# Attention and two MoE layers on one core: transposes of the layer norm's input and of w3 on fp32r-typed operands

## The chip, the cores and the metric

The kernel runs on one core of a Trainium2 chip. The metric is the device time of one execution in microseconds (us), as the median over runs. A measurement of this kernel can tell about 0.3% (some 3.8 us) from no change.

## The reference

All inputs and outputs are float32 (the MoE weights arrive as float64 and are rounded to float32 by the kernel).

```python
def _attn_ref(q, k, v):                      # q, k, v: (8, 8, 576, 64)
    k_p = k.reshape(B, H, Sp, 8, D).mean(axis=3); v_p = ...   # pooled by 8
    attn = softmax(scale * q @ k_p^T)
    return attn @ v_p

def _moe_ref(x, w_in, w_out, g_ln):          # x: (4608, 512), w_in: (512, 1024)
    h = x @ w_in
    solu = h * softmax(h)
    ln = (solu - mean) / sqrt(var + 1e-06) * g_ln
    return ln @ w_out

def _moe2_ref(x, w1, w2, w3, w_out):         # w3: (1024, 1024)
    return ((x @ w1) * (x @ w2) @ w3) @ w_out
```

## The kernel before, in words

Three stages follow each other. TensorE multiplies most matrices as fp32r (one pass) after each fp32 operand has been split into a high and a low fp32r part, three products each; a few products and all transposes run on plain fp32 operands.

**Stage one (to about 640 us)** runs attention, the first MoE layer and the conversion of weights together. Work goes by units of 256 tokens, 18 in all (`Unit`, lines 617 to 655), each of two `Rows` of 128 tokens (lines 567 to 605). A row's product with w_in fills the PSUM tile `h` (`chunk`, line 588: 24 matmuls of 512 columns in four chunks of six). `exp` (line 592) writes the tile `e` (128x1024 fp32), `solu` (line 600) turns `e` on VectorE (line 603) into the layer norm's input, and ScalarE squares it for the variance (line 605). `Unit.transpose(i, hf)` (line 622) transposes half `hf` of row `i`: four 128x128 TensorE transposes of `e` into the PSUM tile `lt` (line 631), a ScalarE copy to `lnh` (line 634) and, one slot later, a VectorE subtraction to `lnl` (line 635). `Unit.chunk` (line 637) multiplies `lnh` and `lnl` with the second weight (lines 645 to 647, 256 columns each) into `x`, which `store` (line 651) copies to `xo` and sends to DRAM. The first quarter of that product needs half 0 of both rows, the second quarter half 1.

The order of stage one on TensorE and on SP, which issues every DMA, is the program's order: a table `events` holds functions by slot, 16 slots to a unit (`put`, `after`, lines 129 to 134; the loop at line 784). A slot's events run first, then one chunk of heavy work: row 0's `h` in slots 0 to 3, `x` in 4 to 7, row 1's `h` in 8 to 11, `x` in 12 to 15. The four transposes of unit u stand in slots 0 to 3 of the next 16 (line 738). VectorE, ScalarE and GpSimd get their order from the scheduler of the framework, which sets it when the program is built. SP issues in order and stands at a DMA whose data or buffer isn't ready. In the same slots the kernel rounds float64 weights, 128x512 at a time (`Rounded`, line 151): a load into `f64` (three buffers, line 157), `cvm` and `cvb` steps on ScalarE (line 170) and VectorE (lines 173 to 182), a sum on GpSimd, a store to DRAM (line 255). Of the attention's own work this text names `q` loads and their transposes `pq`, scores `sc`, exponentials `ea`, the transposes `pt` and `px` of the probabilities, and the product `av`.

**Stage two (about 642 to 710 us)** folds w3 into w_out2: `w3_T(m)` (line 850) loads two 128x512 pieces of w3 into `stg`, transposes each by four TensorE transposes into `pw` (line 857) and splits it; `wf_rows` (line 861) multiplies, 24 matmuls of 512 columns per m. **Stage three** does the second MoE layer and isn't touched.

Of the kernel before, what the change touches and what calls it, by code (L numbers as in the profile page):

```python
# [8 lines left out]
F32 = mybir.dt.float32  # L9
F32R = mybir.dt.float32r  # L10
I32 = mybir.dt.int32
U32 = mybir.dt.uint32
AF = mybir.ActivationFunctionType
# [5 lines left out]
def attention_moe_kernel(  # L19
# [25 lines left out]
    nc = tc.nc  # L45

    B, H, S, D = q.shape
    P = 128
    C = H * D
    NP = H // 2  # L50
    F = w_in.shape[1]
# [15 lines left out]
    const = ctx.enter_context(tc.tile_pool(name="const", bufs=1))  # L67
# [5 lines left out]
    def bank(name):  # L73
        return PS.tile([P, 512], F32, tag="ba", name=name, bufs=3)

    def bankm(name):
        return PS.tile([P, 512], F32, tag="bm", name=name, bufs=3)
# [4 lines left out]
    ident = const.tile([P, P], F32, tag="ident", name="ident")  # L82
    make_identity(nc, ident)
    negid = const.tile([P, P], F32R, tag="negid", name="negid")
    nc.scalar.activation(negid, ident, AF.Copy, scale=-1.0)

    mask8 = const.tile([P, H], F32, tag="mask8", name="mask8")
    m16 = const.tile([P, 16], F32, tag="m16", name="m16")
# [10 lines left out]
    def split(hi, lo, src):  # L99
        nc.scalar.activation(hi, src, AF.Copy)  # L100
        nc.vector.tensor_tensor(lo, src, hi.bitcast(F32), ALU.subtract)
# [7 lines left out]
    def piece(w, i, width=512):  # L109

        n = w.shape[1] // width
        return w[(i // n) * P : (i // n) * P + P, (i % n) * width : (i % n) * width + width]
# [10 lines left out]
    SLOTS = 16  # L123
# [5 lines left out]
    def put(slot, fn, *args, first=5):  # L129
        assert now is None or slot > now  # L130
        events.setdefault(slot, []).append((first, len(events.get(slot, ())), fn, args))

    def after(d, fn, *args, first=3):
        put(now + d, fn, *args, first=first)
# [16 lines left out]
    class Rounded:  # L151
# [7 lines left out]
        def words(self):  # L159
            return A.tile([P, 512, 2], I32, tag="f64", name="f64", bufs=3)  # L160
# [88 lines left out]
    f32w = {}  # L249
# [317 lines left out]
    class Rows:  # L567
# [32 lines left out]
        def solu(self):  # L600

            st, e = self.s, self.e
            nc.vector.scalar_tensor_tensor(e, self.hv, -1.0 / F, e, ALU.mult, ALU.mult, accum_out=st[:, 2:3])
            sq = M2.tile([P, F], mybir.dt.bfloat16, tag="sq", name="sq" + self.nm, bufs=1)
            nc.scalar.activation(sq, e, AF.Square, bias=st[:, 2:3], scale=-1.0 * F, accum_out=st[:, 3:4])

    def out_scale():

        s, ss = ST[:, :, 1], ST[:, :, 3]
        nc.vector.tensor_scalar(kap, s, 1e-9, None, ALU.add)  # L610
        nc.vector.tensor_tensor(kap, kap, kap, ALU.mult)
        nc.vector.tensor_scalar(kap, kap, LNEPS * F, None, ALU.mult)
        nc.vector.tensor_tensor(kap, kap, ss, ALU.add)
        nc.vector.tensor_scalar(kap, kap, 1.0 / F, None, ALU.mult)
        nc.vector.reciprocal(kap, kap)

    class Unit:
# [4 lines left out]
        def transpose(self, i, hf):  # L622
            if (i, hf) == (0, 0):
                self.th, self.tl = [
                    M2.tile([P, FC, U], F32R, tag=t, name=f"{t}{self.u}", bufs=1) for t in ("lnh", "lnl")
                ]
            ln = self.rows[i].e
            pt = bankm(f"lt{self.u}_{i}_{hf}")
            for f in range(4):
                f0 = (4 * hf + f) * P  # L630
                nc.tensor.transpose(pt[:, f * P : f * P + P], ln[:, f0 : f0 + P], ident)  # L631
            fs, cs = slice(4 * hf, 4 * hf + 4), slice(i * P, i * P + P)
            hi, lo, src = self.th[:, fs, cs], self.tl[:, fs, cs], pt.rearrange("p (f n) -> p f n", f=4)
            nc.scalar.activation(hi, src, AF.Copy)  # L634
            after(1, lambda: nc.vector.tensor_tensor(lo, src, hi.bitcast(F32), ALU.subtract), first=0)  # L635
# [30 lines left out]
    T0 = (8, 13)  # L666
# [66 lines left out]
    for un in units:  # L733
        s_ = SLOTS * un.u
        if un.u >= 2 * B:
            put(s_ - 4, un.rows[0].split_x)
        for n in range(4):
            put(s_ + SLOTS + n if un.u else T0[n % 2] + n // 2, un.transpose, n % 2, n // 2, first=1)

    mid = ExitStack()  # L740
    M2 = R = o2 = first_raw = first_w3 = None
# [22 lines left out]
    def w3_pair(m):  # L764
        return [R.tile([P, FC, P], F32R, tag="w3" + t, name=f"w3{t}{m}", bufs=2) for t in "hl"]
# [18 lines left out]
    with tc.manual_schedule(engines={mybir.EngineType.PE, mybir.EngineType.SP}):  # L784
        for s_ in range(min(events), SLOTS * (NU + 1) + 2):
# [3 lines left out]
            u, c = s_ // SLOTS, s_ % SLOTS  # L789
            kind, n = HEAVY[c], c % 4  # L790
# [59 lines left out]
    def w3_T(m):  # L850
        th, tl = w3_pair(m) if m else first_w3
        for i in range(2):
            t = R.tile([P, 512], F32, tag="stg", name="stg", bufs=4)
            nc.sync.dma_start(t, piece(f32w["w3f"], 2 * m + i))
            pw = bank(f"pw{m}_{i}")
            for c in range(4):
                nc.tensor.transpose(pw[:, c * P : c * P + P], t[:, c * P : c * P + P], ident)
            split(th[:, 4 * i : 4 * i + 4], tl[:, 4 * i : 4 * i + 4], pw.rearrange("p (c n) -> p c n", c=4))
        return th, tl

# [9 lines left out]

    BLOCKS_AT = (0, 2, 4, 5)
    nxt = w3_T(0)
    for m in range(FC):
        cur = nxt
        if m + 1 < FC:
            nxt = w3_T(m + 1)
        ow = wf_rows(m, cur)
        if m < FC - 1:
            split(wf[0][:, m], wf[1][:, m], ow)
        if m in BLOCKS_AT:  # L880
            i = BLOCKS_AT.index(m)
            split_blocks(i // 2, i % 2, load_blocks(i // 2, i % 2) if i else first_raw)
# [3 lines left out]
    M2 = ctx.enter_context(tc.tile_pool(name="mlpb", bufs=2, reuse_waits="tile"))  # L886
# [201 lines left out]
```

## Time and profile before

| | before |
|---|---|
| median of 3 runs | 1275.96 us (1274.64 to 1278.98) |
| the profiled execution | 1277.2 us |
| its span | 1275.4 us |
| TensorE matmul busy | 1230.8 us, 97% of the span |
| VectorE, ScalarE, GpSimd busy | 63%, 41%, 32% |
| mean granted TensorE clock | 0.994 |
| DMA | 109.43 MB, q1 busy 29.6% of 16 engines |

The span is the time between the first and the last instruction of the profiled execution; 1.8 us lie around it. The profile has a list of groups of instructions by line, a timeline in order of time, a list of waits (which engine stood still, and what ended that), and the chain: the work that ended last, followed back from the last instruction through whatever released each step. In tile names buffer numbers are left out (`e`, `lt`, `f`). Matmuls are pipelined, so a matmul's own duration is longer than its distance to the next one's start; what a matmul costs in a stream is that distance.

### The profile page before, as it was taken

Reading aid. Unit: us, or ns where it says so; the run is one execution under the profiler, and the core shown is the slowest. Engines: PE = TensorE matmul, PEld = TensorE weight load, DVE = VectorE, ACT = ScalarE, POOL = GpSimd, SP = SyncE. Lnnn points to the kernel's source line nnn. Section 1 sums busy time; section 2 is a strip of 40 time slices with the busy share of each in tenths; the row PEclk is TensorE's granted clock in tenths of the full one; section 3 lists DMA queues with packets and bytes.
Section 4 is the critical chain, followed back from the end, with each engine's and each line's share of the span. In section 5 each row is a group of like instructions: output and inputs, shape, how many; then the busy total and the mean of one; then the engine's idle time right before and its main releaser. Section 6 shows DMA issues by size and latency. Waiting matters only on the chain.

```text
span 1275.4 us, 21828 instructions
## 1 busy us (share of the span) xinstructions
PE 1230.8 (97%) x8278; PEld 1124.8 (88%) x8278; DVE 807.3 (63%) x1595; ACT 525.1 (41%) x1480; POOL 406.6 (32%) x497
## 2 busy tenths in 40 slices
PE   7879999999999999999999999999999999999998
PEld 5669889988988898998988899999999999999997
DVE  6879778777878787755357555545454545454544
ACT  5554666666656666644354221212121212121211
POOL 3332534342525253210000141515152424242411
PEclk9999999999999999999999999999999999999999
DMA  9564546454546464214033102010101010101000
GB/s 236 121 135 115 156 111 164 117 158 133 166 132 167 116 167 116 87 42 140 35 128 111 33 1 67 1 67 1 67 1 67 2 67 1 67 1 66 13 22 34
DMA packets 85754, 109.43 MB, mean 86 GB/s; under 512 B 43664, under 2 KB 43664, under 8 KB 85648
## 3 DMA queue, kind: packets, MB, share of 16 engines
q1 hardware_dynamic: 85648, 108.03, 29.6%
q8 instruction: 65, 1.06, 0.4%
q14 instruction: 41, 0.34, 0.1%
HBM read 78.65 MB, written 29.36 MB: 85 GB/s over the span
## 4 chain that ended last, share of the span: by engine, by line
PE 77%; DVE 9%; DMA 5%; ACT 5%; issue 2%; SPq 1%; POOL 0%; DVEq 0%; ACTq 0%; POOLq 0%
PE h L588 11%; PE p L948 9%; PE p L950 9%; PE p L949 9%; PE acc L994 5%; PE acc L997 5%; PE acc L996 5%; PE x L646 3%; PE x L647 3%; PE x L645 3%; DMA f<-in_moe_w_dram 3%; PE av L557 2%; PE lt L631 2%; ACT ea L473 2%; PE sc L452 1%
## 5 line engine op out<-in xcount | busy, mean ns | idle before, releaser
L968 POOL TENSOR_TENSOR a<-a,b 128x256 f32<-128x256 f32 x72 | 52.9, 735 | 477.5 <-DVE b L967 477.5
L952 ACT ACTIVATE p<-p 128x256 f32<-128x256 f32 x72 | 27.9, 387 | 397.4 <-PE p L950 365.4
L645 PE MATMUL x<-lnh,gwh 128*128 128x256 f32 x576 | 166.4, 289 | 0.0
L646 PE MATMUL x<-lnl,gwh 128*128 128x256 f32 x576 | 163.0, 283 | 2.1 <-DVE lnl L635 2.1
L647 PE MATMUL x<-lnh,gwl 128*128 128x256 f32 x576 | 162.8, 283 | 0.0
L189 POOL TENSOR_TENSOR cvb<-cvb,cvm 128x512 f32<-128x512 f32 x46 | 60.9, 1325 | 186.3 <-DVE cvm L182 180.6
L473 ACT ACTIVATE ea<-sc,mx 128x72 f32<-128x72 f32 x320 | 98.6, 333 | 36.7 <-DVE mx L470 36.7
L997 PE MATMUL acc<-wfl,ph 128*128 128x512 f32 x288 | 113.0, 393 | 0.0
L646 PEld LDWEIGHTS x<-lnl,gwh 128*128 128x128 f32 x576 | 110.1, 191 | 3.3 <-DVE lnl L635 2.3
L996 PE MATMUL acc<-wfh,ph 128*128 128x512 f32 x288 | 112.9, 392 | 0.0
L645 PEld LDWEIGHTS x<-lnh,gwh 128*128 128x128 f32 x576 | 110.0, 191 | 1.0 <-DVE lnl L635 0.2
L647 PEld LDWEIGHTS x<-lnh,gwl 128*128 128x128 f32 x576 | 110.0, 191 | 0.0
L967 DVE TENSOR_TENSOR b<-b,p 128x256 f32<-128x256 f32 x72 | 30.2, 419 | 123.0 <-PE p L950 123.0
L588 PE MATMUL h<-winh,xh 128*128 128x512 f32 x288 | 99.0, 425 | 0.0
L588 PE MATMUL h<-winl,xh 128*128 128x512 f32 x288 | 89.9, 393 | 0.0
L588 PE MATMUL h<-winh,xl 128*128 128x512 f32 x288 | 89.6, 392 | 0.0
L948 PE MATMUL p<-th,w1h 128*128 128x256 f32 x288 | 81.6, 283 | 1.1 <-ACT p L952 1.1
L994 PE MATMUL acc<-wfh,pl 128*128 128x512 f32 x288 | 82.3, 392 | 0.0
L635 DVE TENSOR_TENSOR lnl<-lt,lnh 128x512 fp32r<-128x512 f32 x72 | 49.2, 686 | 51.3 <-ACT lnh L634 50.9
L949 PE MATMUL p<-th,w1h 128*128 128x256 f32 x288 | 81.5, 283 | 0.0
L950 PE MATMUL p<-th,w1l 128*128 128x256 f32 x288 | 81.5, 283 | 0.0
L956 DVE TENSOR_TENSOR u<-p,p 128x256 f32<-128x256 f32 x72 | 30.3, 421 | 77.3 <-PE p L950 76.2
(201 smaller groups left out, 3725.1 us busy)
## 6 DMA issues: line engine op xcount, KB each, us to landing
f<-in_moe_w_dram SPq DMA_DIRECT2D x32, 512.0 KB, 5.8
x2d<-xo SPq DMA_DIRECT2D x36, 256.0 KB, 2.0
xq<-x2d SPq DMA_DIRECT2D x36, 256.0 KB, 3.7
out_dram<-ot SPq DMA_DIRECT2D x36, 256.0 KB, 2.7
kv<-in_k_dram SPq DMA_DIRECT2D x32, 256.0 KB, 3.7
q<-in_q_dram SPq DMA_DIRECT2D x32, 256.0 KB, 7.5
kv<-in_v_dram SPq DMA_DIRECT2D x32, 256.0 KB, 3.6
f<-in_moe_w_out_dram SPq DMA_DIRECT2D x16, 512.0 KB, 6.0
```

The lines of the kernel that those rows point to most:

```text
L189: self.engine.tensor_tensor(self.f, self.f, self.m.bitcast(F32), ALU.add)
L473: nc.scalar.activation(e[0:n, x], half[a][:, h], AF.Exp, bias=mx[0:n, x : x + 1], scale=1.0, accum_out=sm[0:n, x : x + 1],)
L588: nc.tensor.matmul(self.ph[:, a], s_[:, c], w_[:, c, a * 512 : a * 512 + 512], start=first, stop=last)
L645: nc.tensor.matmul(o, gw[0][:, f, ws], self.th[:, f], start=(f == 0), stop=False)
L646: nc.tensor.matmul(o, gw[0][:, f, ws], self.tl[:, f], start=False, stop=False)
L647: nc.tensor.matmul(o, gw[1][:, f, ws], self.th[:, f], start=False, stop=(f == FC - 1))
L948: nc.tensor.matmul(o, wh[:, c, fsl], th[:, c], start=c == 0, stop=False)
L949: nc.tensor.matmul(o, wh[:, c, fsl], tl[:, c], start=False, stop=False)
L950: nc.tensor.matmul(o, wl[:, c, fsl], th[:, c], start=False, stop=c == 1)
L994: nc.tensor.matmul(accs[t], pl[:, ts], wh, start=False, stop=(fc == FC - 1))
L996: nc.tensor.matmul(accs[t], ph[:, ts], wh, start=(fc == 0), stop=False)
L997: nc.tensor.matmul(accs[t], ph[:, ts], wl, start=False, stop=False)
```

## The change

The transposes of the layer norm's input and of w3 take fp32r-typed operands: a second identity, `identr`, is typed fp32r, and the transposes' outputs are viewed as fp32r. An operand typed fp32r has to come from a tile of that type. For w3 the staging tile itself is now typed fp32r and the load writes it through an fp32 view. The layer norm's input is written by VectorE in fp32 and is read by ScalarE for the variance; so each row gets a tile `er` (128x1024 fp32r, two buffers), filled from `e` by two DMAs of 128x512 (256 KB each) through an fp32 view, issued by SP one slot after `solu`: 72 DMAs of 18.9 MB together. The four transposes of a unit are reordered: row 0's two halves, then row 1's two, where before half 0 of both rows came first. The numbers of the transposes, copies and subtractions stay.

```diff
--- before.py
+++ after.py
@@ -83,6 +83,8 @@
     make_identity(nc, ident)
     negid = const.tile([P, P], F32R, tag="negid", name="negid")
     nc.scalar.activation(negid, ident, AF.Copy, scale=-1.0)
+    identr = const.tile([P, P], F32R, tag="identr", name="identr")
+    nc.scalar.activation(identr, ident, AF.Copy)
 
     mask8 = const.tile([P, H], F32, tag="mask8", name="mask8")
     m16 = const.tile([P, 16], F32, tag="m16", name="m16")
@@ -603,6 +605,14 @@
             nc.vector.scalar_tensor_tensor(e, self.hv, -1.0 / F, e, ALU.mult, ALU.mult, accum_out=st[:, 2:3])
             sq = M2.tile([P, F], mybir.dt.bfloat16, tag="sq", name="sq" + self.nm, bufs=1)
             nc.scalar.activation(sq, e, AF.Square, bias=st[:, 2:3], scale=-1.0 * F, accum_out=st[:, 3:4])
+            after(1, self.words, first=2)
+
+        def words(self):
+
+            self.er = M2.tile([P, F], F32R, tag="er", name="er" + self.nm, bufs=2)
+            for i in range(2):
+                cs = slice(i * 512, i * 512 + 512)
+                nc.sync.dma_start(self.er[:, cs].bitcast(F32), self.e[:, cs])
 
     def out_scale():
 
@@ -624,11 +634,11 @@
                 self.th, self.tl = [
                     M2.tile([P, FC, U], F32R, tag=t, name=f"{t}{self.u}", bufs=1) for t in ("lnh", "lnl")
                 ]
-            ln = self.rows[i].e
+            ln = self.rows[i].er
             pt = bankm(f"lt{self.u}_{i}_{hf}")
             for f in range(4):
                 f0 = (4 * hf + f) * P
-                nc.tensor.transpose(pt[:, f * P : f * P + P], ln[:, f0 : f0 + P], ident)
+                nc.tensor.transpose(pt[:, f * P : f * P + P].bitcast(F32R), ln[:, f0 : f0 + P], identr)
             fs, cs = slice(4 * hf, 4 * hf + 4), slice(i * P, i * P + P)
             hi, lo, src = self.th[:, fs, cs], self.tl[:, fs, cs], pt.rearrange("p (f n) -> p f n", f=4)
             nc.scalar.activation(hi, src, AF.Copy)
@@ -735,7 +745,7 @@
         if un.u >= 2 * B:
             put(s_ - 4, un.rows[0].split_x)
         for n in range(4):
-            put(s_ + SLOTS + n if un.u else T0[n % 2] + n // 2, un.transpose, n % 2, n // 2, first=1)
+            put(s_ + SLOTS + n if un.u else T0[n // 2] + n % 2, un.transpose, n // 2, n % 2, first=1)
 
     mid = ExitStack()
     M2 = R = o2 = first_raw = first_w3 = None
@@ -850,11 +860,11 @@
     def w3_T(m):
         th, tl = w3_pair(m) if m else first_w3
         for i in range(2):
-            t = R.tile([P, 512], F32, tag="stg", name="stg", bufs=4)
-            nc.sync.dma_start(t, piece(f32w["w3f"], 2 * m + i))
+            t = R.tile([P, 512], F32R, tag="stg", name="stgr", bufs=4)
+            nc.sync.dma_start(t.bitcast(F32), piece(f32w["w3f"], 2 * m + i))
             pw = bank(f"pw{m}_{i}")
             for c in range(4):
-                nc.tensor.transpose(pw[:, c * P : c * P + P], t[:, c * P : c * P + P], ident)
+                nc.tensor.transpose(pw[:, c * P : c * P + P].bitcast(F32R), t[:, c * P : c * P + P], identr)
             split(th[:, 4 * i : 4 * i + 4], tl[:, 4 * i : 4 * i + 4], pw.rearrange("p (c n) -> p c n", c=4))
         return th, tl
```

TensorE at the end of unit 5 and the start of unit 6 (`lt6_i_hf` is unit 6, row i, half hf; `h7_0` is row 0 of unit 7), before:

```order
L647 MATMUL x2_5_1_3347<-lnh5_3019,gwl_104 128x256
L631 MATMUL lt6_0_0_3449<-ident_66,e6_0_3140 128x128 x4
L588 MATMUL h7_0_3463<-winh_101,xh7_3284 128x512 x2
...
L631 MATMUL lt6_1_0_3471<-ident_66,e6_1_3317 128x128 x4
...
L631 MATMUL lt6_0_1_3501<-ident_66,e6_0_3140 128x128 x4
...
L631 MATMUL lt6_1_1_3515<-ident_66,e6_1_3317 128x128 x4
L518 MATMUL pt8_1_3521<-ident_66,pr8_1_3479 128x128 x4
```

and now:

```order
L657 MATMUL x2_5_1_3388<-lnh5_3057,gwl_106 128x256
L641 MATMUL lt6_0_0_3493<-identr_73,er6_0_3220 128x128 x4
L590 MATMUL h7_0_3507<-winh_103,xh7_3325 128x512 x2
...
L641 MATMUL lt6_0_1_3515<-identr_73,er6_0_3220 128x128 x4
...
L641 MATMUL lt6_1_0_3545<-identr_73,er6_1_3425 128x128 x4
...
L641 MATMUL lt6_1_1_3559<-identr_73,er6_1_3425 128x128 x4
L520 MATMUL pt8_1_3565<-ident_66,pr8_1_3523 128x128 x4
```

Row 1's first transpose has moved from the second to the third place; nothing else moved on TensorE.

SP in unit 5 (`e5_0` is row 0 of unit 5; `f64` a weight piece, `kv4` keys of the batch after), before:

```order
L655 DMA x2d_100<-xo3_1_2638 128x512
L426 DMA q7_1_2666<-in_q_dram 128x8x64
L157 DMA f64_2668<-in_moe2_w3_dram 128x1024
L255 DMA w3f_119<-cvb_2642 128x512
L429 DMA QL_115<-in_q_dram 64x8x64
L157 DMA f64_2762<-in_moe2_w3_dram 128x1024
L300 DMA kv4_0_2796<-in_k_dram 64x2x512 x2
L308 DMA KL8_117<-in_k_dram 64x1x512
L655 DMA x2d_100<-xo4_0_2828 128x512
```

and now:

```order
L665 DMA x2d_102<-xo3_1_2670 128x512
L428 DMA q7_1_2698<-in_q_dram 128x8x64
L159 DMA f64_2700<-in_moe2_w3_dram 128x1024
L257 DMA w3f_121<-cvb_2674 128x512
L431 DMA QL_117<-in_q_dram 64x8x64
L615 DMA er5_0_2787<-e5_0_2755 128x512 x2
L159 DMA f64_2797<-in_moe2_w3_dram 128x1024
L302 DMA kv4_0_2831<-in_k_dram 64x2x512 x2
L310 DMA KL8_119<-in_k_dram 64x1x512
L665 DMA x2d_102<-xo4_0_2863 128x512
```

The copy of row 0 stands ahead of a weight load and the key loads, which now wait with it for `e5_0`.

ScalarE around row 1 of unit 5, before:

```order
L440 ACTIVATE qT7_1_2873<-pq7_1_2868 128x512
L170 ACTIVATE cvm_3045<-f64_2881 128x512
L597 ACTIVATE e5_1_2898,ST_77<-h5_1_2841,ST_77 128x1024
L473 ACTIVATE ea7_1_2944,sm7_1_2943<-sc7_1_0_2907,mx7_1_2942 128x72 x4
L473 ACTIVATE ea7_1_2944,sm7_1_2943<-sc7_1_1_2910,mx7_1_2942 128x72 x2
```

and now:

```order
L172 ACTIVATE cvm_2922<-f64_2797 128x512
L475 ACTIVATE ea7_0_2885,sm7_0_2884<-sc7_0_0_2866,mx7_0_2883 128x72 x4
L475 ACTIVATE ea7_0_2885,sm7_0_2884<-sc7_0_1_2869,mx7_0_2883 128x72 x4
L442 ACTIVATE qT7_1_2908<-pq7_1_2903 128x512
L599 ACTIVATE e5_1_2933,ST_79<-h5_1_2876,ST_79 128x1024
L475 ACTIVATE ea7_1_2979,sm7_1_2978<-sc7_1_0_2942,mx7_1_2977 128x72 x4
```

The scheduler has moved the weight step that stood ahead of `e5_1` elsewhere, and put the one on `f64_2797` ahead of the exponentials `ea7_0`.

## Rows read from the trace of the kernel before

**Rows 1.** The page: the span.
```profile
span 1275.4 us, 21828 instructions
```
**Rows 2.** Busy time by stretch: us, PE (x), PEld, DVE, ACT, POOL, PEclk, DMA share, GB/s.
```profile
250.00:350.00 100.00, 97.77 (x680) 89.62 (x679) 79.71 (x149) 64.86 (x221) 46.20 (x61) 1.00 0.53 148
```
**Rows 3.** The chain that ended last, shares of the span by line.
```profile
PE h L588 11%; PE p L948 9%; PE p L950 9%; PE p L949 9%; PE acc L994 5%; PE acc L997 5%; PE acc L996 5%; PE x L646 3%; PE x L647 3%; PE x L645 3%; DMA f<-in_moe_w_dram 3%; PE av L557 2%; PE lt L631 2%; ACT ea L473 2%; PE sc L452 1%
```
**Rows 4.** Timeline of PE in unit 6: start us, us, engine, line, operation, count.
```profile
304.96 0.29 PE L647 MATMUL x<-lnh,gwl 128*128 128x256 f32 x1
305.09 0.60 PE L631 MATMUL lt<-ident,e 128*128 128x128 f32 x4
305.44 0.71 PE L588 MATMUL h<-winh,xh 128*128 128x512 f32 x2
305.99 0.63 PE L588 MATMUL h<-winl,xh 128*128 128x512 f32 x2
...
306.92 0.60 PE L631 MATMUL lt<-ident,e 128*128 128x128 f32 x4
...
308.74 0.60 PE L631 MATMUL lt<-ident,e 128*128 128x128 f32 x4
```
**Rows 5.** Groups of PE by line and shape: count, busy us, mean ns, idle before.
```profile
L452 PE MATMUL sc<-bdt,qT 128*128 128x144 f32 x320 | 48.1, 293 | 3.0 <-ACT qT L440 3.0
L631 PE MATMUL lt<-ident,e 128*128 128x128 f32 x288 | 43.8, 276 | 6.2 <-ACT qT L440 5.7 <-DVE lnl L635 0.6
```
**Rows 6.** Timeline of PE early in stage one.
```profile
15.31 0.33 PE L374 MATMUL pkl<-ident,KL 128*128 128x128 f32 x1
...
17.86 1.14 PE L452 MATMUL sc<-bdt,qT 128*128 128x144 f32 x8
```
**Rows 7.** Timeline of PEld, the loading of stationary operands, there.
```profile
15.31 0.14 PEld L374 LDWEIGHTS pkl<-ident,KL 128*128 128x128 f32 x1 [0.17 <-issue]
15.37 0.47 PEld L437 LDWEIGHTS pq<-ident,q 128*128 128x128 f32 x4
```
**Rows 8.** Timeline of PE: fp32r products of 320 columns.
```profile
295.09 0.31 PE L557 MATMUL av<-ptl,VBDh 128*128 128x320 f32 x1
295.24 0.31 PE L557 MATMUL av<-pth,VBDl 128*128 128x320 f32 x1
```
**Rows 9.** Timeline of PE at the start of stage two.
```profile
653.71 1.91 PE L857 MATMUL pw<-ident,stg 128*128 128x128 f32 x16
```
**Rows 10.** Timeline of DVE: the layer norm's input, rows 5_0, 6_1 and 17_1.
```profile
248.71 1.22 DVE L603 SCALAR_TENSOR_TENSOR e<-h,e 128x1024 f32<-128x1024 f32 x1
...
299.79 1.22 DVE L603 SCALAR_TENSOR_TENSOR e<-h,e 128x1024 f32<-128x1024 f32 x1
...
636.83 1.22 DVE L603 SCALAR_TENSOR_TENSOR e<-h,e 128x1024 f32<-128x1024 f32 x1
```
**Rows 11.** DMA issues: count, KB each, median us from issue to landing.
```profile
f<-in_moe_w_dram SPq DMA_DIRECT2D x32, 512.0 KB, 5.8
x2d<-xo SPq DMA_DIRECT2D x36, 256.0 KB, 2.0
```
**Rows 12.** Timeline of PE at the end of stage one, unit 17.
```profile
639.43 1.51 PE L631 MATMUL lt<-ident,e 128*128 128x128 f32 x12
...
642.09 0.39 PE L645 MATMUL x<-lnh,gwh 128*128 128x256 f32 x1
```
**Rows 13.** Waits of PE: waiting group, releaser, us in total, times, longest.
```profile
PE lt L631 <- ACT qT L440: 5.7, 6, 2.5
```
**Rows 14.** Timeline of SP in unit 5.
```profile
241.18 0.64 SPq L157 DMA_DIRECT2D f<-in_moe_w_dram  x1
```
**Rows 15.** Timeline of ACT in unit 5.
```profile
256.27 0.32 ACT L473 ACTIVATE ea<-sc,mx 128x72 f32<-128x72 f32 x1 [1.56 <-DVE mx L470]
...
263.33 0.68 ACT L170 ACTIVATE cvm<-f 128x512 f32<-128x512 f32 x1 [4.03 <-DMA f<-in_moe_w_dram]
263.92 1.10 ACT L597 ACTIVATE e<-h,ST 128x1024 f32<-128x1024 f32 x1
```

## The prediction, made before the changed kernel had run

> **What bounds the kernel now.** I read the views in this order. The page gives the span [rows 1]; the profiled execution took 1277.2 us, 1.2 us over the median of the runs, and the sum below is made against it. Busy time by stretch says which engine fills stage one: over 100 us in its middle TensorE is busy for 97.77, VectorE for 79.71, ScalarE for 64.86 [rows 2]. So little idle time is left on TensorE that every nanosecond taken out of its stream counts, unless another engine then ends last. The chain says how often that is: it consists mostly of TensorE's products, but 3% of it is weight loads by DMA, and `lt` has 2% [rows 3]. 2% of 1275.4 is 25.5 us. All 72 groups of four `lt` transposes cost 72 x 0.44 = 31.7 us (next paragraph), so about 0.8 of them lie on the path. Then the timeline of TensorE, for what one transpose costs in the stream.
>
> **What a transpose costs now.** Sixteen in a row last 1.91 us [rows 9]; one by itself has a duration of 0.27 [rows 5], so one follows the other by (1.91 - 0.27) / 15 = 0.109 us. From one group of four in unit 6 to the next are 1.83 us, with six products of 512 columns between [rows 4]; less 4 x 0.109 that leaves 0.232 per product. Two things could set the 0.109: the stream of 128 columns, or the loading of the stationary operand. The loading: a transpose that started on an idle engine lasted 0.33 instead of 0.27, and the next one's load began 0.06 after its own [rows 6, 7]; so a transpose waits 0.06 for its weights, not 0.109. The stream: eight fp32 products of 144 columns last 1.14, one of them 0.29 [rows 5, 6], so they follow each other by 0.121, 0.84 ns a column; the transposes, at 0.85 ns a column, lie on the same line. fp32r products need 0.15 at 320 columns [rows 8] and 0.232 at 512, about 0.43 ns a column more for each further column: half. I read the transposes as fp32 streams that pass the array twice, with the weights hidden behind them.
>
> The Trainium skill speaks against that and against the change: TensorE: Matmul & The Clock Gate, section LDWEIGHTS (loading the stationary operand), has every load of 128 columns take 128 / 1.2 = 107 ns whatever the operand is. By it 0.109 would be the load, the type would be worth 2 ns at most, and the sum below would lose its whole gain; the 0.06 of the trace decides for me.
>
> **What an fp32r transpose costs.** No row shows one. From above: nothing is gained if type doesn't matter (0.109), or 0.12 if it streams no faster and gets the fixed part of the fp32r products on top (0.15 - 320 x 0.00043 = 0.012). From below: the 0.06 of its load. In between, the line through the fp32r products at 320 and 512 columns gives 0.15 - 192 x 0.00043 = 0.067 at 128. I take 0.067, the same kind of operand on the same engine; saved are 0.042 each.
>
> **Layer norm transposes.** In a group of four the last doesn't gain. The product after it shows why: its pair lasts 0.71 where the next pair lasts 0.63 [rows 4], so its stream starts at 305.52, 0.10 after the last transpose's start (305.09 + 3 x 0.109): its own weights begin to load only then and take that long, whatever the transpose does. So three of four gain in 68 groups, and 15 of the 16 that unit 17 runs in a row: 219 x 0.042 = 9.2 us, of which 0.8 are on the path: **7.4 us**.
>
> **w3 transposes.** 64 in batches of 16 and six of 8, with nothing but products on TensorE between; all but the last of each gain: 57 x 0.042 = **2.4 us**, all on the path, since TensorE hardly waits there.
>
> **The copies.** 72 DMAs of 256 KB. In steady units the layer norm's input of row 1 is ready at 299.79 + 1.22 = 301.01 and now first used where the third `lt` group stands, at 308.74 [rows 4, 10]: 7.7 us. 256 KB landed in 2.0, 512 KB in 5.8 [rows 11]; so the pair lands in time, at no cost. Without that cover each microsecond over 7.7 is paid once a unit. In unit 17 there is no such distance: the input is ready at 638.05 [rows 10]; the third group stands at 639.43 + 8 x 0.109 = 640.30 and `x` starts at 642.09 [rows 12]. A landing in 2.0 costs nothing, in 5.8 it makes the third group 3.5 late, in 3.9, the middle, 1.6. Nothing else is left for TensorE there, so I count **1.6 us** lost (0 to 3.5). The new order of halves gives row 1's first half the place that its second half had, with the same distance to its use; I cost it at nothing, covered by the slot between. The extra DMA traffic of 18.9 MB and the one ScalarE copy of the identity at the start go beside other work.
>
> **What moves on the other queues.** On SP the copy of `e5_0` now stands ahead of a weight load and key loads, which were issued from 241.18 on [rows 14] and now wait for `e5_0` until 248.71 + 1.22 = 249.93 [rows 10]. On ScalarE the weight step that waited 4.03 us for its DMA ahead of `e5_1` [rows 15] is gone from there, but another, on the load that is now late, stands ahead of `ea7_0`. The first could give back up to 5.7 us, what TensorE waits at `lt` for ScalarE in all [rows 13]; the second is the rival below. I set both at nothing.
>
> **The sum**: 1277.2 - 7.4 - 2.4 + 1.6 = 1269.0 for the profiled execution; less the 1.2 by which it lies over the median, 1267.8. With 0.06 per transpose (0.049 saved), everything on the path and no stall in unit 17 it is 13.5 less than 1276.0, and 1257 with the 5.7 on top; with half of the `lt` gain on the path and the dear end in unit 17 it is 1272.5.
>
> **Rivals.** *The type makes no difference (0.22).* The transposes stream 128 columns at half rate whatever the operand, or an fp32r transpose loads its weights as slowly as the products do, 0.10. For it: no fp32r transpose has been seen, and 0.109 is what 128 columns at 1.2 GHz take, too. Against: the granted clock is 1.00 in the stretch [rows 2], which is 2.4 GHz, and transposes lie on the line of the other fp32 streams. Nothing is gained, unit 17 is paid: 1276.0 + 1.6 = 1277.6; with 0.12 per transpose 3.0 more. The Trainium skill, TensorE: Matmul & The Clock Gate, Part 4: PE-mode transpose, has a bf16 transpose in a kernel at about 275 ns and says that transposes don't run at the full clock; the fp32 ones here have 276 [rows 5], which would speak for this rival; no run here has a bf16 transpose.
>
> *Slower: the late loads (0.15).* The weight load behind the copy is issued about 251.2 (two copies issued at 0.64 each, the time of an issue [rows 14]) and lands 5.8 later, at 257.0, or up to 262.8 if it also has to wait out the copy. The weight step takes 0.68 [rows 15], and `ea7_0`, which started at 256.27, starts at 257.7 to 263.5: 1.4 to 7.2 late. Its results go through VectorE and GpSimd to TensorE's `pt`. The pattern comes once in two units, seven times. If half of the middle, 2.2 us, reaches TensorE each time, that is 15 us: 1283. It decides for slower from 1.7 us a time. For it: the same wait of ScalarE is already on the chain [rows 3, 15]. Against: VectorE and GpSimd have time left there, and the scheduler placed the steps with the later loads in view.
>
> **How the numbers follow.** Forecast 0.60, type without effect 0.22, late loads 0.15, something else 0.03. About 0.3%, 3.8 us, is what a measurement can tell: faster means under 1272.1, slower over 1279.8. Faster holds nearly all of the forecast, 0.57; the same holds most of the first rival and the forecast's upper end, 0.22; slower the second rival, the first with 0.12, and the rest, 0.21. The range reaches from near the forecast's low end over the first rival, 1259 to 1281; late loads lie mostly above. The forecast's own range is 1259 to 1272.5.
>
> **What would show it.** Sixteen w3 transposes in about 1.28 us (0.27 + 15 x 0.067) instead of 1.91, and a unit's groups closer by 0.13 each; 1.91 again means the first rival. TensorE waiting for `er` in unit 17 alone, by 1 to 3 us; waits in every unit would make the copies the cause. `ea` waiting on ScalarE behind `cvm`, and `pt` on TensorE later than before, would be the second rival. The prediction is wrong if transposes keep their distance, or if TensorE's idle time in stage one grows by more than the transposes lose.

## The result: 1.1% slower, and the profile after

The changed kernel takes 1293.39 us (median; 1287.92 to 1294.20) against 1275.97, a ratio of 1.0112 with a 95% interval of 1.0090 to 1.0133. The prediction was 1267.8: wrong in sign, and above its range. The profiled execution took 1294.18 us. Its page (the span, the chain by engine, the copies):

```profile
span 1292.4 us, 21978 instructions
...
PE 62%; DVE 15%; DMA 7%; ACT 7%; issue 4%; POOL 3%; SPq 2%; POOLq 0%; ACTq 0%; DVEq 0%
...
er<-e SPq DMA_DIRECT2D x72, 256.0 KB, 2.4
```

and the chain by engine on the page of before:

```profile
PE 77%; DVE 9%; DMA 5%; ACT 5%; issue 2%; SPq 1%; POOL 0%; DVEq 0%; ACTq 0%; POOLq 0%
```

TensorE's share of the chain falls from 77% to 62%; VectorE, DMA, ScalarE and GpSimd take it over. So the end is now set more often by what TensorE waits for. The copies themselves are nearly as cheap as forecast: 2.4 us from issue to landing, against 2.0 [rows 11].

**The transposes did get cheaper.** Groups of instructions of after, against [rows 5], then TensorE's timeline in unit 6 against [rows 4], and twelve w3 transposes in a row against [rows 9]:

```profile
L641 PE MATMUL lt<-identr,er 128*128 128x128 f32 x288 | 35.1, 246 | 8.9 <-ACT qT L442 6.9 <-DVE ptx L532 1.2 <-DVE lnl L645 0.4
```

```profile
315.31 0.46 PE L641 MATMUL lt<-identr,er 128*128 128x128 f32 x4
...
317.06 0.46 PE L641 MATMUL lt<-identr,er 128*128 128x128 f32 x4
...
672.54 1.20 PE L867 MATMUL pw<-identr,stgr 128*128 128x128 f32 x12 [0.44 <-ACT xo L664]
```

Four in a row last 0.46 instead of 0.60. One by itself lasts 0.24 to 0.25, so they follow each other by about (0.46 - 0.24) / 3 = 0.073, in the run of twelve by (1.20 - 0.24) / 11 = 0.087, where fp32 had 0.109. From one group to the next are 1.75 us instead of 1.83: 0.08 a group, 72 x 0.08 = 5.8 us in all. TensorE waited for a copy (`er`) once in the whole run, 0.3 us, in unit 17.

**The loss is ahead of all that.** Stage two begins at 671.6 instead of 653.7 and the end of the span is 17.0 later: everything is lost in stage one. By the start of a unit's first product of `x` the changed kernel is 6.2 us late in unit 0, 7.7 in unit 1, 16.5 in unit 13 and 16.1 in unit 17; stage two begins 17.9 late. So some 8 us are lost at the start, some 9 bit by bit in the units after it, and 2 behind unit 17. SP's waits, of before and of after (waiting group, releaser, us in total, times, longest):

```profile
SPq L655 <- ACT xo L654: 390.1, 36, 15.2
```

```profile
SPq L615 <- DVE e L605: 261.2, 34, 13.3
SPq L615 <- DVE ptx L532: 21.3, 1, 21.3
SPq L665 <- ACT xo L664: 59.6, 28, 10.1
```

SP has little to do and stands most of the time. Before, it stood at the stores of `x`; the loads behind a store went out as soon as it was through, up to half a unit ahead. Now it stands at the copies (L615), waiting for VectorE's `e`, and the loads behind a copy wait with it. The second line of after is the wait at the very first copy, which the list puts down to another step of VectorE; with one more of 6.9 us SP stands 36 times and 289 us at copies. SP's timeline around 380 us of before, then of after:

```profile
374.23 0.68 SPq L157 DMA_DIRECT2D f<-in_moe_w_dram  x1
375.00 1.35 SPq L300 DMA_DIRECT2D kv<-in_k_dram  x2
...
386.60 0.32 SPq L655 DMA_DIRECT2D x2d<-xo  x1
```

```profile
393.22 1.12 SPq L615 DMA_DIRECT2D er<-e  x2
394.38 2.00 SPq L159 DMA_DIRECT2D f<-in_moe_w_dram  x1
396.43 1.35 SPq L302 DMA_DIRECT2D kv<-in_k_dram  x2
...
398.55 0.39 SPq L665 DMA_DIRECT2D x2d<-xo  x1
```

The same weight load and key loads were issued 12.4 us ahead of the store of `x`, and are now 4.2 ahead of it. What follows from that load stands in the chain of after (start, us, what), and from another one further on:

```profile
394.38 6.64 DMA f<-in_moe_w_dram
401.11 0.67 ACT cvm L172
401.77 0.86 ACT ea L475 x6
...
404.20 0.50 ACT qT L442
404.74 1.25 PE sc L454 x8
```

```profile
434.13 5.54 DMA f<-in_moe_w_dram
...
439.75 0.68 ACT cvm L172
...
440.46 0.70 DVE cvm L175
441.16 0.33 DVE xl L103
441.49 0.14 DVE X L566
...
441.77 0.98 PE av L559 x5
```

The weight step `cvm` waits for the load; in the first piece ScalarE's `ea` and `qT` stand behind it, in the second VectorE's `xl` and `X`, and TensorE waits for these. TensorE's waits from 160 to 640 us, before and after:

```profile
PE pt L518 <- DVE X L564: 5.8, 6, 1.1
PE lt L631 <- ACT qT L440: 3.2, 5, 1.1
PE x L646 <- DVE lnl L635: 2.1, 1, 2.1
```

```profile
PE lt L641 <- ACT qT L442: 6.9, 5, 2.0
PE av L559 <- DVE X L566: 5.3, 4, 1.5
PE pt L520 <- DVE X L566: 3.3, 6, 0.6
```

At the start it happens once, at a higher price. SP's timeline of before, then of after:

```profile
59.23 1.25 SPq L300 DMA_DIRECT2D kv<-in_v_dram  x2
...
62.45 0.53 SPq L221 DMA_DIRECT2D f<-in_moe_w_out_dram  x1
```

```profile
62.60 1.19 SPq L615 DMA_DIRECT2D er<-e  x2
63.89 1.35 SPq L302 DMA_DIRECT2D kv<-in_v_dram  x2
...
67.18 0.58 SPq L223 DMA_DIRECT2D f<-in_moe_w_out_dram  x1
```

The first copy stands ahead of the value loads and of a load of w_out, which come 4.7 us later; `nm`, the product that needs w_out's weights, waits 4.6 us for them instead of 1.7, and unit 0's `x` begins 6.2 us late. Of these, 1.4 were there ahead of the first copy: the first product of `h` begins at 50.68 instead of 49.23 (in the other kernels here that run in the framework's order between 49.6 and 52.0).

### The profile page after: what moved, and what is told of

It is laid out like the page before. It is cut to its first block, busy times and chain, and to the rows that moved or that the text cites. A ratio compares the mean times of both kernels' runs of the same rounds, so it can differ in the third digit from the quotient of the medians.

```text
span 1292.4 us, 21978 instructions
## 1 busy us (share of the span) xinstructions
PE 1232.3 (95%) x8278; PEld 1119.3 (87%) x8278; DVE 801.5 (62%) x1595; ACT 523.7 (41%) x1481; POOL 407.2 (32%) x497
## 4 chain that ended last, share of the span: by engine, by line
PE 62%; DVE 15%; DMA 7%; ACT 7%; issue 4%; POOL 3%; SPq 2%; POOLq 0%; ACTq 0%; DVEq 0%
PE p L958 9%; PE p L960 9%; PE p L959 9%; PE acc L1004 5%; PE h L590 5%; PE acc L1007 5%; PE acc L1006 5%; DMA f<-in_moe_w_dram 4%; ACT ea L475 3%; DVE e L605 2%; PE x L656 2%; PE x L657 2%; PE x L655 2%; DVE ST L598 2%; PE av L559 1%
## 5 line engine op out<-in xcount | busy, mean ns | idle before, releaser
L495 POOL TENSOR_TENSOR pr<-ea,sm 128x512 f32<-128x512 f32 x40 | 44.4, 1109 | 123.1 <-DVE sm L491 91.6
```

## The experiments

Theory 1: SP stands at the copies, and the loads behind them are late. Theory 2: the framework, which sets the order of VectorE, ScalarE and GpSimd with SP's stand in view, chose a worse order. Theory 3: the 18.9 MB slow the other transfers. Theory 4: the new order of halves. Ratios are to the kernel before, measured beside each kernel, with 95% intervals.

**One part alone: w3.** Only the edits of `w3_T` and `identr`.

> The kernel before with the w3 part alone: 64 w3 transposes on fp32r-typed operands, layer norm transposes, order of halves and everything else as before. All theories of the loss put it into stage one, so none expects a loss here: about 1275.3 us, 0.7 under the kernel before, which is what stage two won between its first transpose and stage three in the changed kernel. If the w3 part won its full 2.4 us of the prediction, 1273.6; if it lost anything, the 17 us of the changed kernel would not all lie in stage one.

Measured: 1276.42 us, 0.9991 (0.9975 to 1.0007). No loss; a gain of this size can't be told from none. Stage three begins 50.05 us after the first w3 transpose in the changed kernel, 50.72 before: 0.7 won; here it is 49.79, 0.9 won.

**One part alone: the order of halves.** Only the line `put(... un.transpose ...)`.

> The kernel before with the new order of halves alone (row 0's two halves, then row 1's two); no copies, all transposes fp32. VectorE, ScalarE and GpSimd keep the order of the kernel before apart from the halves' own steps. Theory 1: nothing, 1276 us (ratio 0.998 to 1.002). Theory 4 (the order of halves costs the time): 1290 or more.

Measured: 1278.34, 1.0005 (0.9986 to 1.0023). Theory 4 falls.

**The copies without their use.**

```diff
-            ln = self.rows[i].er
+            ln = self.rows[i].e
-  nc.tensor.transpose(pt[...].bitcast(F32R), ln[...], identr)
+  nc.tensor.transpose(pt[...], ln[...], ident)
```

> The changed kernel with the copies as they are, but the layer norm transposes run on the fp32 tile e with the fp32 identity; nothing reads the copies. Theory 1 (SP stands at the copies until e is ready, and the loads behind them come late): the loss stays and the gain of the transposes goes, 1293.4 plus 7 to 9, so 1300 to 1302 us. Theory of a wait of TensorE for the copies themselves: no one waits for them any more, so at most 1277. Theory 3 (the 18.9 MB of copies slow the other transfers): 1300 as by theory 1.

Measured: 1295.53, 1.0146 (1.0112 to 1.0179). The copies alone lose more than the whole change, if not the 1300 us expected; no one waits for them.

**The wait without the bytes.** The kernel above, with

```diff
-  nc.sync.dma_start(self.er[:, cs].bitcast(F32), self.e[:, cs])
+  nc.sync.dma_start(self.er[0:16, cs].bitcast(F32), self.e[0:16, cs])
```

> The kernel of copies_fp32_transposes with copies of 16 of the 128 partitions only (32 KB each in place of 256 KB), nothing reads them. Orders on TensorE, VectorE, ScalarE and GpSimd are those of copies_fp32_transposes, row for row; SP still stands at each copy until e is ready, but 7/8 of the bytes are gone. Theory 1 (SP stands, loads behind it are late): the same time as copies_fp32_transposes, 1293 to 1297 us (ratio to the kernel before about 1.0146). Theory 3 (bytes of the copies slow other transfers): 1276 to 1280.

Measured: 1295.81, 1.0129 (1.0101 to 1.0157). With an eighth of the bytes and row for row the same order on the engines the loss is the same, within the intervals: theory 3 falls. The cause is the wait at the copies, together with the order on VectorE and ScalarE that was built around it, which is the same in both kernels.

**The bytes without the wait.** `words` copies the row before, `src = units[self.u - (self.i == 0)].rows[1 - self.i].e`, except for the first row.

> The changed kernel, but each copy reads the tile e of the row before it, which has long been ready when SP comes to it: the same number of copies on SP, the same bytes, the same fp32r transposes, which transpose another row's data (so the layer norm's product is left without its right input). Theory 1: SP never stands for e, the loads come as in the kernel before and the transposes' gain shows, 1264 to 1270 us. Theory 3 (bytes): 1290 to 1295.

Measured: 1284.85, 1.0051 (1.0034 to 1.0067): half of the loss is gone, not all, a miss. SP stands at the stores of `x` again (330.3 us, 36 times). Most of the rest is the start, since SP still stands at the first row's copy (20.3 us): unit 0's `x` begins 6.6 us late here too. The other part is in steady units: TensorE's waits from 160 to 640 us are 15.6 us, 11.3 before, the largest `lt` for `qT` (6.2 instead of 3.2), though SP doesn't stand at copies there. The order on VectorE and ScalarE differs from before.

**The copies later on SP**, right ahead of the store of `x`, where SP would stand anyway.

```diff
-            after(1, self.words, first=2)
+            after(3, self.words, first=2)
```

> The changed kernel with the copies of a row two slots later in the program (three slots after solu in place of one), where they stand right ahead of the store of x, so that the loads of the two slots between go out before SP can stand at e. Nothing else is edited; copies, bytes and transposes stay. Theory 1 (loads behind the copy are late): nearly all of the loss goes and the gain of the transposes shows: 1276.0 less about 7 less 0.7, so 1266 to 1271 us. Theory 3 (the bytes of the copies slow other transfers): no change, 1290 to 1295. Theory 4 (the order of halves): no change either.

Measured: 1282.91, 1.0037 (1.0018 to 1.0055): again between the theories. The loads are early again: the weight load of the piece shown above goes out 12.1 us ahead of the store of `x`, as before (12.4), although SP stands at the copies for nearly as long as in the changed kernel (243.5 us). So the standing by itself makes no load late; what counts is what stands behind it. But TensorE's `sc` now waits for `xl`, 8.5 us in five times, because in this build `xl` stands behind a weight step and a `kp` reduction on VectorE.

**The copies on another queue**, ScalarE's.

```diff
-  nc.sync.dma_start(self.er[:, cs].bitcast(F32), self.e[:, cs])
+  nc.scalar.dma_start(self.er[:, cs].bitcast(F32), self.e[:, cs])
```

> The changed kernel with the copies issued by ScalarE in place of SP; all else as in the changed kernel. Theory 1: SP no longer stands at e, the loads come as early as before, 1266 to 1273 us (the upper end if 72 issues of DMAs take ScalarE time on its way to TensorE). Theory 3 (bytes): 1290 to 1295. Theory 4 (order of halves): 1290 to 1295.

Measured: 1266.41, **0.9919** (0.9898 to 0.9941): faster than before, 2% under the changed kernel, by one word. ScalarE's timeline shows why the copy holds up nothing there:

```profile
412.62 1.15 ACT L607 ACTIVATE sq<-e,ST 128x1024 bf16<-128x1024 f32 x1
412.68 1.13 ACTq L615 DMA_DIRECT2D er<-e  x2
```

It is issued right behind the start of `sq`, which waits for the same `e`: ScalarE has that wait in any case. SP's list of waits has SP back at the stores:

```profile
SPq L665 <- ACT xo L664: 350.7, 36, 16.1
```

and TensorE's waits from 160 to 640 us are shorter than before:

```profile
PE lt L641 <- ACT qT L442: 2.9, 2, 2.2
PE sc L454 <- DVE X L566: 1.1, 1, 1.1
```

**The same with the old order of halves.**

> The kernel of copies_by_ScalarE_queue with the order of halves of the kernel before (half 0 of both rows first), so that row 1's copy has one slot less before its first use. If the new order is needed as cover, TensorE waits for er in each unit: the input is ready at 301.0, a copy lands 2.4 later, the second group of transposes stands at 306.9, so nothing should wait and the time should be that of copies_by_ScalarE_queue, 1265 to 1268 us; if the landing of the pair takes over 5.9, 1 us a unit more, up to 1284.

Measured: 1266.12, **0.9906** (0.9887 to 0.9926). The new order isn't needed as cover. This version and the one above beat both kernels.

**Whose gain is it?** The kernel with ScalarE's queue, transposes on fp32 `e`.

> The kernel of copies_by_ScalarE_queue with the layer norm transposes on the fp32 tile e again; the copies go out on ScalarE's queue as there, and nothing reads them. The 12 us that copies_by_ScalarE_queue has over the kernel before are either the transposes' (theory A: the 219 that can gain, by 0.03 to 0.042 each, and the w3 part), or partly those of another order of the steps on VectorE and ScalarE that the framework set when it built that kernel (theory B: TensorE's waits for X ahead of pt, 5.8 us in the kernel before, are gone there). Theory A: ratio to the kernel before 0.998 to 1.001, 1275 to 1278 us. Theory B: 0.994 to 0.996, 1269 to 1272.

Measured: 1289.49, 1.0094 (1.0064 to 1.0125). Both theories miss. The twins are 1.75%, 22 us, apart, and the transposes are worth 6. VectorE's timeline has what the rest comes from:

```profile
255.84 1.40 DVE L176 TENSOR_SCALAR cvb<-cvm 128x512 int32<-128x512 int32 x1
257.27 0.69 DVE L182 SCALAR_TENSOR_TENSOR cvb<-f,cvb 128x512 int32<-128x512 int32 x1
...
259.07 1.88 DVE L334 TENSOR_REDUCE kp<-kv 128x128 f32<-128x1024 f32 x1
260.87 1.27 DVE L103 TENSOR_TENSOR xl<-av,xh 128x512 fp32r<-128x512 f32 x2
```

TensorE's waits from 160 to 640 us, its timeline there, and busy time by stretch, its columns as in [rows 2]:

```profile
PE sc L454 <- DVE xl L103: 14.7, 6, 3.0
```

```profile
261.60 0.76 PE L454 MATMUL sc<-bdt,qT 128*128 128x144 f32 x4 [2.58 <-DVE xl L103]
```

```profile
258.00:262.00 4.00, 1.42 (x12) 1.20 (x11) 3.97 (x5) 0.60 (x1) 2.56 (x4) 1.00 0.66 192
262.00:268.00 6.00, 6.00 (x24) 4.83 (x24) 3.11 (x6) 3.37 (x18) 1.97 (x5) 0.72 0.99 252
```

In this build a second weight step and `kp` stand ahead of `xl`, so `sc` waits up to 3.0 us, six times, and behind the wait of 2.58 shown the granted clock is 0.72 over 6 us. The four longer of these waits (2.6 to 3.0 us) are followed by the same, 0.66 to 0.72 over 6 to 10 us. That adds up: TensorE's waits from 160 to 640 us are 15.7 us here and 5.9 in the twin, 9.8 more; the mean granted clock of the whole run is 0.986 instead of 0.993, which over 1287.9 and 1265.5 us is some 9 us of full speed, an estimate; the transposes are 5.8. That is about 25, where the spans differ by 22. So an order alone, with no one standing at a copy, can move this kernel by over 1%.

**One order for all.** To tell theory 2 from theory 1, VectorE, ScalarE and GpSimd were held to the program's order in units 2 to 14.

```diff
-    with tc.manual_schedule(engines={PE, SP}):
-        for s_ in range(min(events), SLOTS * (NU + 1) + 2):
+    with tc.manual_schedule(engines={PE, SP}):
+        for s_ in range(min(events), 32):
...
+    with tc.manual_schedule(engines={PE, SP, DVE, Activation, Pool}):
+        for s_ in range(32, 230):
...
+    with tc.manual_schedule(engines={PE, SP}):
+        for s_ in range(230, SLOTS * (NU + 1) + 2):
```

> The kernel before, with VectorE, ScalarE and GpSimd also held to the program's order from slot 32 to 229 (units 2 to 14), in place of the framework's order. It is the reference for the three other pinned kernels, whose orders on these engines in that stretch are the same but for the halves' steps. Its own time depends on how good the program's order is: between 1270 and 1310 us.

Measured: 1352.23, 1.0590 (1.0566 to 1.0615).

> The changed kernel with the same pinned order. Theory 1 (the loads behind the copies are late while it runs, whatever the order): 8 to 17 us over pinned_before. Theory 2 (SP's stand changed the order that the framework set when it built the kernel, and the order costs the time): about 4 us of the start, less 5 for the transposes, so at pinned_before or up to 3 under it.

Measured: 1358.39, 1.0639 (1.0615 to 1.0664), 6.2 us over pinned_before, between the theories.

> The kernel of copies_by_ScalarE_queue with the same pinned order. By both theories only the transposes are left: 72 groups by 0.077 us are 5.5, the w3 part 0.7, the start gives back about 1: 4 to 7 us under pinned_before, in place of the 12 that the framework's orders gave.

Measured: 1353.78, 1.0596 (1.0568 to 1.0625), no gain: a miss.

> The kernel of ScalarE_copies_fp32_transposes (1.0094 of the kernel before) with the same pinned order. Theory 2: its loss was the order of VectorE, so it is at pinned_before, within 3 us. If copies on ScalarE's queue cost time of themselves, it stays 10 us or more over pinned_before.

Measured: 1354.52, 1.0609 (1.0579 to 1.0639), 2.3 over pinned_before: the loss of its unpinned twin doesn't come back, which fits the order as its cause. For the rest the four are no good judges, because the program's order is a bad one: TensorE is busy for 421 of the 480 us from 160 to 640, where before it was 469, so neither cheaper transposes nor late loads in steady units reach the end. What pinned_after loses it has lost by unit 1, whose first product of `x` starts at 152.24 instead of 143.43; after that it loses nothing more.

**The start alone.** The changed kernel with

```diff
-  nc.sync.dma_start(self.er[...], self.e[:, cs])
+  (nc.sync if self.u else nc.scalar).dma_start(self.er[...], self.e[:, cs])
```

> The changed kernel with the four copies of unit 0 alone issued by ScalarE, the other 68 by SP as they are. In the changed kernel the first copy stands on SP from slot -3 of the program on, ahead of key, value, query and weight loads of the start, and unit 0 ends 6.2 us later than before, of which 1.4 are there ahead of the first copy. Theory 1 with two places (start and steady units): 4 to 5 us less than the changed kernel, 1288 to 1290. If the start only shifts a wait that comes anyway: 1292 to 1294.

Measured: 1284.69, 1.0049 (1.0030 to 1.0067). Four of the 72 copies make about 8 us of the loss (1.0112 - 1.0049 = 0.0063 of 1276, by the intervals 4 to 12), more than the 4 to 5 that I expected. Unit 0's `x` begins 0.3 us ahead of before, not 6.2 late; in unit 17 it is 8.2 late, where the changed kernel is 16.1.

> The kernel of copies_later_on_SP with the four copies of unit 0 issued by ScalarE. Two separate losses by theory 1: the start (8.7 us in the changed kernel, as unit0_copies_by_ScalarE showed) and the steady units (SP stands ahead of the loads). Here neither is left: what remains over copies_by_ScalarE_queue is the order of VectorE's steps that this build has. The start was 5.4 late here, so 4 to 5 us less than copies_later_on_SP: 1277 to 1279, a ratio to the kernel before of 0.999 to 1.001. If the start were only one more wait that later ones swallow: 1282 to 1283.

Measured: 1280.16, 1.0022 (1.0006 to 1.0037). Only 2 us less than copies_later_on_SP, within the intervals of the two. Unit 0's `x` still begins 2.9 us late here, against 5.4 there: with the copies at their later place, the four at the start account for only half of that. What the rest comes from is not shown.

**A third queue**, GpSimd's (`nc.gpsimd.dma_start`).

> The changed kernel with the copies issued by GpSimd in place of SP. Theory 1 alone (SP no longer stands): as copies_by_ScalarE_queue, 1264 to 1270 us. If GpSimd's own work (sums of the weights, products of probabilities, on TensorE's way) is held up by issuing, or by standing at e, or if the framework's order turns out badly again: 1275 to 1290.

Measured: 1304.33, 1.0199 (1.0179 to 1.0219), the slowest with the framework's order. GpSimd's waits:

```profile
POOL er L615 <- DVE e L605: 64.4, 13, 13.3
POOL er L615 <- issue: 61.9, 7, 10.3
```

Here GpSimd stands at the copies, up to 13.3 us, and what stands behind are the products of the probabilities and the weights' sums. So it need not be SP; but how this reaches TensorE is not shown: its largest wait from 160 to 640 us is `sc` for `xl`, 11.1 us, behind a step of VectorE, and another order is in this build too.

## Why the prediction was wrong

**What bounds the kernel, and what a transpose costs: right.** The type matters; the first rival is out. Only the size was off: 0.067 was forecast, 0.073 in groups of four and 0.087 in the run of twelve measured; a group saves 0.08 where 3 x 0.042 = 0.126 was forecast, so the layer norm's term is 5.8 us in all for 9.2. The Trainium skill, TensorE: Matmul & The Clock Gate, section LDWEIGHTS (loading the stationary operand), has 128 / 1.2 = 107 ns for a load; the fp32r transposes, each with a load of its own, follow each other by 0.073 and 0.087 us, so the trace disagrees, as the prediction held.

**w3: 2.4 forecast.** 0.7 shows in stage two, and the run of that part alone can't be told from no change. At the 0.087 measured the 57 transposes would gain 1.3, and stage two has a wait of 0.44 at its fifth transpose that it didn't have before.

**Unit 17's stall: 1.6 forecast, nearly met by luck.** TensorE's timeline of after, and busy time by stretch behind it:

```profile
655.39 0.81 PE L641 MATMUL lt<-identr,er 128*128 128x128 f32 x8
656.50 0.51 PE L641 MATMUL lt<-identr,er 128*128 128x128 f32 x4 [0.31 <-DMA er<-e]
...
658.14 0.36 PE L655 MATMUL x<-lnh,gwh 128*128 128x256 f32 x1 [0.16 <-DVE lnl L645]
```

```profile
660.00:662.00 2.00, 2.00 (x11) 2.00 (x11) 0.00 (x0) 0.00 (x0) 0.00 (x0) 0.50 0.00 0
```

From the first transpose to `x` are 2.75 us, against 2.66 [rows 12]: only about 0.1 is lost there, with a wait for `er` of 0.3, where 1 to 3 were forecast. But from that `x` to stage two are 13.50 us instead of 11.62, another 1.9: behind the three short waits of unit 17 the granted clock fell to 0.50, which is 1.2 GHz, and products of 256 columns followed each other by 0.21 us instead of 0.12. The prediction has no such term.

**The copies at no cost: right as to TensorE's wait for them, and beside the point.** They do land in time. What the step didn't ask is who is queued behind them on SP.

**"I set both at nothing": this step failed.** The prediction saw that the copy of `e5_0` stood ahead of a weight load and key loads, and let two effects of opposite sign and unknown size cancel. It looked at one copy where SP stands 36 times: 289 us of waiting at copies in place of that at the stores. And it took the 7.7 us that TensorE has in hand as the cover for the copy, while the loads behind it need a cover of their own, which the stores had left them and the copies took away. The second rival had the mechanism, at 1283 with 0.15; it counted seven places in steady units and left out the start, where the first copy holds back loads that TensorE is about to need: about 8 us by itself. Its "VectorE and GpSimd have time left" was wrong too: it is on VectorE that the late step stands ahead of `xl`.

**The order of the other engines.** The prediction took "the scheduler placed the steps with the later loads in view" as a point for the forecast. The twins on ScalarE's queue show that this is a risk of its own: 22 us apart, and the pair is level again once the order is pinned (where, though, even the 5.8 us of the transposes don't show). What stays open is how much of the changed kernel's loss in steady units came from loads that are late while it runs, and how much from the order built around them; wait_without_bytes shows that both hang on the wait, not which of them is larger. No run had the order of before together with SP's waits.

**The gain of ScalarE's queue** (0.9919, some 10 us) is thus not the transposes' alone: they and w3 give 5.8 + 0.7 = 6.5; the rest fits TensorE's waits from 160 to 640 us, 11.3 us in all before and 5.9 here, which came with another order; no run separates the two.

## What to carry to other kernels

Before adding a DMA that waits for computed data, list what stands behind it on the issuing queue, and ask how far ahead those loads were issued so far; put it on a queue whose next instruction waits for the same data anyway. Count the first occurrence separately from the steady ones. Where a scheduler sets an order, a change of a wait is also a change of the order on the other engines: compare builds whose orders are the same before a difference is put down to the edit.

## What was not expected of the hardware

A wait of TensorE can cost more than itself: behind the wait of 2.58 us shown for ScalarE_copies_fp32_transposes the granted clock was 0.72 over 6 us, so part of that stretch ran at 1.2 GHz in place of 2.4. In unit 17 of the changed kernel three waits of 0.2 to 0.5 us within 2 us were followed by a clock of 0.50 over 2 us; before, one wait of 0.55 in the same place was not (1.00 over the 2 us behind it). And ScalarE's queue issued two copies of 256 KB in 1.13 us beside `sq`, which took the 1.15 us it has in the kernel before as well (mean 1154 ns).
